# Row layout of the first 512 tokens and new engine orders in a fused linear-attention and ReLU kernel

## The chip, the cores and the metric

The kernel runs on one core of one Trainium2 chip. The metric is device time in microseconds (us), as the median of plain runs. Beside them there is one execution with the hardware profiler on; rows of the profile come from that one.

## What is computed

Two blocks read the same x of 2048 tokens by 512 (A_x; the input B_x is not used), and a gate per token mixes them. All tensors are bf16.

```python
x = A_x
g = sigmoid((x * gate_w).sum(-1, keepdims=True))
# a: 32 heads of 16; q, k, v = x @ wqkv
pq = q @ w_phi; pk = k @ w_phi                      # per head
phi_q = concat(softmax(pq), softmax(-pq))           # 32 features per head
phi_k = concat(softmax(pk), softmax(-pk))
kv = sum over tokens of phi_k * v;  z = sum over tokens of phi_k
a = ((phi_q @ kv) / (phi_q @ z + 1e-6)) @ wo
# b: b = max(x @ w1, 0) @ w2                         (w1 512 x 1376, w2 1376 x 512)
out = g * a + (1 - g) * b
```

The order of tokens matters nowhere except that a row of the output belongs to the same row of x: the sums over tokens don't depend on it.

## The kernel before, in words

**Tiles.** The 2048 tokens are 16 tiles of 128, in four chunks of 512. XT holds x transposed (512 features on partitions in four blocks, tokens along the row). The first chunk is loaded plainly (two loads, xa0 and xa1, each with two neighbouring rows of x per partition, lines 277 to 282) and transposed on PE (xt0a to xt3b, line 325; copied out by ACT and DVE, xe, lines 337 and 339). The other three chunks come by transposing loads (x1, x2, x3, line 269). Tile m of the first chunk thus holds every second row of a block of 256, and the function rows(m) writes the output of these tiles back to the same rows (line 348).

**The steps,** with the names that the text uses, a number standing for a tile, job or chunk:

- v (line 374): values of a tile, copied out by ACT (ve, 379).
- f1, f0 (356): w_phi folded into the key and query weights; these weights come by transposing loads wkT and wqT. Evictions fe (317, 319).
- h (397): x @ w1, one block of 128 hidden features by 512 tokens, ReLU by ACT into HT (rl, 415). The last 96 features and the gate's dot product come in hr (405), with rr on ACT and a transposing load ht (426) from SBUF to SBUF.
- pr (454): the folded projection of a job (two tiles, or one at the end; k0 to k8 for keys, q0 to q8 for queries). Then ev (ACT, 479), mx and mn (DVE, 483, 485), t1 and t2 (POOL, 492), ex (ACT, 497), sm and rc (DVE, 499, 503, 523), and nm (POOL, 506 for keys, 529 for queries; ra at 525 before it).
- kv (513): sum of key features by values over all tokens in two PSUM banks; kn and kz (544, 546) copy it out once kv15 is done.
- tq (532): transposing load of a query tile's features; nd (556): numerator and denominator in two halves; rd and o (562, 564) divide and gate; to (569): transposing load of that into OT.
- b (577): HT @ W2 of a tile, eleven matmuls, and a (583): OT @ WO, four matmuls into the same PSUM bank; oe (628) evicts with the factor 1 - g, and st (631) stores, both on ACT. The last tile is split into two parts (598, 609, 619, 622).

**What sets the order.** Each step is a task with an engine and dependencies. Nothing is scheduled when the kernel runs: the dictionary ORDER (line 17) holds the order of every engine's queue, written out: sp (all loads, 54), pool, act, dve and pe. `emit` (127) goes through each queue and puts a semaphore wait ahead of a task whose dependencies lie on other engines. A task that waits holds up all behind it on its engine. The numbers `dur` and `lat` of the tasks are not used to build the program.

**Buffers that tie engines together.** The h units, hr and f0 take the PSUM banks 3, 4, 5 in turn by their number (h0_0 bank 3, h0_1 bank 4, h0_2 bank 5, h0_3 bank 3, and so on); each waits for the eviction of the one before it in that bank. The v of tiles 4 to 15 share bank 2. b and a of tile m use bank 3, 4 or 5 and wait for oe of tile m - 3. nd uses banks 6, 7 and 2 in turn and waits for the o three halves before. Each pr waits for the ev before it (banks 0 and 1).

```python
for s, v in need.items():
    if waited.get(s, 0) < v:
        waited[s] = v
        eng.wait_ge(sems[s], v)
last = t.fn(eng)
last.then_inc(sems[t.sem], 16 if t.dma else 1)
```

Of the kernel before, what the change touches and what calls it, by code (L numbers as in the profile page):

```python
# [15 lines left out]

ORDER = {
    "sp": (
        "xa0 wva xa1 wvb w1a wphi wkT w1b x1 gw w1c wqT x2 x3 w2a w2b ht1 wo ht0 tq1 tq0 tq2 tq3 to0 to1 ht2 to2 "
        "tq4 tq5 to3 tq6 tq7 to4 to5 ht3 tq8 tq9 to6 to7 tq11 tq10 to8 to9 tq12 tq13 to11 to10 tq14 tq15 to12 "  # L20
        "to13 to14 to15 st15_1 "
    ),
    "pool": (
# [5 lines left out]
    ),  # L29
    "act": (  # L30
# [8 lines left out]
    ),  # L39
    "dve": (  # L40
# [10 lines left out]
    ),  # L51
# [10 lines left out]
    ),  # L62
}

# [78 lines left out]
def bass_gated_mix__linear_kernel_hedgehog__dense_activation_relu__prompt_kernel(  # L143
# [11 lines left out]
    x2 = A_x.rearrange("b s d -> (b s) d")  # L155
    o2 = out.rearrange("b s d -> (b s) d")
# [3 lines left out]
    P = 128  # L160
# [20 lines left out]
    with ExitStack() as es:  # L181
# [92 lines left out]

        w1r = B_w1.rearrange("(j p) n -> p j n", p=P)
        wvr = A_wqkv[:, 2 * D:3 * D].rearrange("(j p) n -> p j n", p=P)
        def pair(i):
            return x2[2 * i * P:2 * (i + 1) * P, :].rearrange("(p t) d -> p (t d)", t=2)

        load("xa0", "sp", XN[:, 0:2, :].rearrange("p t d -> p (t d)"), pair(0), dur=0.47, lat=2.25)  # L280
        load("wva", "sp", WV[:, 0:2, :], wvr[:, 0:2, :], dur=0.46, lat=2.55)
        load("xa1", "sp", XN[:, 2:4, :].rearrange("p t d -> p (t d)"), pair(1), dur=0.5, lat=3.2)
        load("wvb", "sp", WV[:, 2:4, :], wvr[:, 2:4, :], dur=0.48, lat=3.75)
        load("w1a", "sp", W1[:, :, 0:512], w1r[:, :, 0:512], dur=0.51, lat=4.75)
# [62 lines left out]

        def rows(m):
            if m < 4:
                i = m // 2  # L350
                return o2[2 * i * P:2 * (i + 1) * P, :].rearrange("(p t) d -> p t d", t=2)[:, m % 2, :]
            return o2[m * P:(m + 1) * P, :]

        def pe_fold(q, s, j, b):
# [105 lines left out]
        for jn, (kind, tiles) in enumerate(jobs):  # L460
# [27 lines left out]
            for tn, M, sg in (("t1", MX, 0), ("t2", MN, 1)):  # L488
                o3 = ap(TS, NTS * 2 * F, ts * 2 * F + sg * GV, [[2 * GV, w * NG], [DH, GH], [1, DH]])
                m3 = ap(M, NSL * 2 * H, sl * 2 * H, [[GH, w * NG], [1, GH], [0, DH]])  # L490
                a3, b3 = (pb3, m3) if sg == 0 else (m3, pb3)
# [27 lines left out]
            else:  # L519
# [29 lines left out]
                for m in tiles:  # L549
# [38 lines left out]
                    if m == NT - 1:  # L588
# [41 lines left out]
                        (f"a{m}", f"go{m // 4}", f"st{m - NOS}" if m >= NOS else None), dur=0.69)  # L630
                    add(f"st{m}", "act", lambda q, m=m: q.dma_start(
                        out=rows(m), in_=OSB[:, m % NOS, :]), (f"oe{m}",), dur=0.39, lat=1.7, dma=True)

        for line in (("warm0", "xt0a", "xt0b", "xt1a", "xt1b", "v0a", "v1a", "xt2a", "xt2b", "xt3a", "xt3b", "warm1",
# [45 lines left out]
```

## Time and profile before

| | before |
|---|---|
| median of 3 plain runs | 151.71 us |
| lowest, highest | 151.42, 151.90 us |
| the profiled execution | 151.17 us |
| its span, first to last instruction | 149.2 us |
| PE, DVE, POOL, ACT busy | 97%, 74%, 74%, 61% |
| TensorE clock granted | 1.00 |
| read from and written to HBM | 4.41 MB, 2.10 MB |

A row of a group or of a timeline names the line of the kernel, the engine, the operation, and out<-in by the program's tensors. PE is the matmul side of TensorE, PEld its weight loads, SPq the queue of SyncE that issues loads. In the chain of work that ended last, each piece has a start, a length and what it was; "issue" is time for which the profile shows no cause. Times are counted from the span's start.

### The profile page before, as it was taken

What the parts mean: (1) busy time and instruction counts of PE and PEld (TensorE: products, weight loads), DVE (VectorE), ACT (ScalarE), POOL (GpSimd) and SP (SyncE); (2) the same over time, 40 slices, a digit from 0 to 9 for tenths busy, and PEclk for the clock granted to TensorE, in tenths of its full rate; (3) what the DMA queues carried; (4) which work ended last, traced back from release to release, by engine and by line L of the source; (5) the groups of instructions that cost most, each with busy time, mean ns of one, the idle gap of its engine ahead of it and who ended that gap; (6) DMA issues with size and microseconds to landing.
All of it is one profiled execution on the core that took longest, in us unless ns stands there. A gap on an engine that the chain in (4) does not pass through costs nothing.

```text
span 149.2 us, 2538 instructions
## 1 busy us (share of the span) xinstructions
PE 144.9 (97%) x968; PEld 73.0 (49%) x984; DVE 110.8 (74%) x169; ACT 91.1 (61%) x127; POOL 109.7 (74%) x73
## 2 busy tenths in 40 slices
PE   7899999999999999999999999999999999999994
PEld 2454444454454645444547445444545454544553
DVE  0542679999995499989569899999979987817501
ACT  3347769997886888966896854476535443303131
POOL 4000599999999999999999999999958795060000
PEclk9999999999999999999999999999999999999999
DMA  5999999500003400000000061847495964787423
GB/s 140 295 199 223 259 166 276 191 0 0 4 2 94 116 7 0 0 0 0 4 0 0 0 141 32 151 104 186 102 172 109 245 156 107 135 208 211 106 73 108
DMA packets 45524, 16.11 MB, mean 108 GB/s; under 512 B 39272, under 2 KB 45256, under 8 KB 45512
## 3 DMA queue, kind: packets, MB, share of 16 engines
q1 hardware_dynamic: 43208, 13.89, 42.3%
q10 hardware_dynamic: 2304, 2.06, 4.3%
q8 instruction: 8, 0.13, 0.4%
q14 instruction: 4, 0.03, 0.1%
HBM read 4.41 MB, written 2.10 MB: 44 GB/s over the span
## 4 chain that ended last, share of the span: by engine, by line
PE 94%; DMA 3%; issue 1%; SPq 1%; DVE 0%
PE PS L577 24%; PE PS L397 23%; PE PS L454 19%; PE PS L374 9%; PE PS L583 9%; PE PS L513 3%; DMA FT<-in_A_x_dram 3%; PE PS L556 3%; PE PS L405 2%; PE PS L598 2%; PE PS L356 1%; PE PS L609 1%; SPq L265 1%; PE PS L325 0%; DVE OSB L619 0%
## 5 line engine op out<-in xcount | busy, mean ns | idle before, releaser
L492 POOL TENSOR_TENSOR TS<-PB,MX 128x1024 bf16<-128x1024 bf16 (+1 forms) x18 | 30.8, 1716 | 13.9 <-DVE MX L483 13.9
L499 DVE TENSOR_REDUCE ZB<-FT 128x128 f32<-128x2048 bf16 (+1 forms) x18 | 36.6, 2037 | 4.6 <-ACT FT L497 4.5
L397 PE MATMUL PS<-XT,W 128*128 128x512 bf16 x155 | 37.7, 379 | 0.3
L577 PE MATMUL PS<-W,HT 128*128 128x512 bf16 (+1 forms) x161 | 37.0, 379 | 0.2
L497 ACT ACTIVATE FT<-TS 128x2048 bf16<-128x2048 bf16 (+1 forms) x18 | 31.0, 1720 | 4.5 <-PE PS L513 2.4
L492 POOL TENSOR_TENSOR TS<-MN,PB 128x1024 bf16<-128x1024 bf16 (+1 forms) x18 | 30.8, 1720 | 0.1
L454 PE MATMUL PS<-WP,XT 128*128 128x512 bf16 x126 | 30.1, 379 | 0.1
L506 POOL TENSOR_TENSOR FT<-FT,SC 128x2048 bf16<-128x2048 bf16 (+1 forms) x9 | 29.5, 3285 | 0.0
L415 ACT ACTIVATE HT<-PS 128x512 bf16<-128x512 f32 x40 | 22.8, 601 | 6.3 <-PE PS L397 6.2
L628 ACT ACTIVATE OSB<-PS,OMG 128x512 bf16<-128x512 f32 x15 | 10.2, 685 | 23.5 <-PE PS L583 23.5
L479 ACT ACTIVATE PB<-PS 128x1024 bf16<-128x1024 f32 (+1 forms) x18 | 16.8, 932 | 12.3 <-PE PS L454 8.1
L577 PEld LDWEIGHTS PS<-W,HT 128*128 128x128 bf16 (+1 forms) x165 | 15.5, 97 | 17.4 <-ACT OSB L628 0.3
L397 PEld LDWEIGHTS PS<-XT,W 128*128 128x128 bf16 x160 | 15.0, 98 | 17.5 <-ACT HT L415 1.0
L483 DVE TENSOR_REDUCE MX<-PB 128x64 bf16<-128x1024 bf16 (+1 forms) x18 | 19.5, 1082 | 5.4 <-ACT PB L479 5.4
L485 DVE TENSOR_REDUCE MN<-PB 128x64 bf16<-128x1024 bf16 (+1 forms) x18 | 19.2, 1075 | 0.3 <-ACT PB L479 0.2
L454 PEld LDWEIGHTS PS<-WP,XT 128*128 128x128 bf16 x128 | 12.1, 98 | 14.0 <-DVE WP L319 0.4
L529 POOL TENSOR_TENSOR FT<-FT,SR 128x1024 bf16<-128x1024 bf16 (+1 forms) x9 | 15.6, 1736 | 0.6
L374 PE MATMUL PS<-WV,XT 128*128 128x512 bf16 x61 | 15.5, 379 | 0.2
L583 PE MATMUL PS<-WO,OT 128*128 128x512 bf16 x58 | 14.4, 378 | 0.1
L564 DVE SCALAR_TENSOR_TENSOR OTM<-PS,EG,RD 128x256 bf16<-128x256 f32 x32 | 14.1, 466 | 0.4
L562 DVE RECIPROCAL RD<-PS 128x16 f32<-128x16 f32 x32 | 7.0, 238 | 8.2 <-PE PS L556 7.9
L379 ACT ACTIVATE VS<-PS 128x512 bf16<-128x512 f32 x16 | 9.5, 607 | 3.0 <-PE PS L374 3.0
(54 smaller groups left out, 96.3 us busy)
## 6 DMA issues: line engine op xcount, KB each, us to landing
out_dram<-OSB ACTq DMA_DIRECT2D x15, 128.0 KB, 2.5
W<-in_B_w_dram SPq DMA_DIRECT2D x1, 1280.0 KB, 8.2
W<-in_B_w_dram SPq DMA_DIRECT2D x2, 512.0 KB, 5.0
FT<-in_A_x_dram SPq DMA_DIRECT2D x2, 256.0 KB, 3.4
WV<-in_A_wqkv_dram SPq DMA_DIRECT2D x2, 256.0 KB, 3.7
WO<-in_A_wo_dram SPq DMA_DIRECT2D x1, 512.0 KB, 4.6
W<-in_B_w_dram SPq DMA_DIRECT2D x1, 352.0 KB, 3.6
PHQ<-FT SPq DMA_TRANSPOSE x16, 2.8
```

Of the source, the lines that this page charges most:

```text
L374: last = q.matmul(PS[:, b, :], XT[:, j, m * P:(m + 1) * P], WV[:, j, :], start=(j == 0), stop=(j == ND - 1))
L397: last = q.matmul(PS[:, b, :], W1[:, j, k * P:(k + 1) * P], XT[:, j, chunk(c)], start=(j == 0), stop=(j == ND - 1))
L415: add(f"rl{a}_{k}", "act", lambda q, a=a, k=k, b=b: q.activation(HT[:, k, chunk(a)], PS[:, b, :], ACT.Relu), (f"h{a}_{k}",), dur=0.6)
L454: last = q.matmul(PS[:, n, :], XT[:, j, m * P:(m + 1) * P], WP[:, s, j, :], start=(j == 0), stop=(j == ND - 1))
L483: add(f"mx_{J}", "dve", lambda q, sl=sl, w=w, i=pbg: q.tensor_reduce(MX[:, sl, 0:w * H], i, AX.X, ALU.max), (f"ev_{J}", old("t1")), dur=0. ...
L485: add(f"mn_{J}", "dve", lambda q, sl=sl, w=w, i=pbg: q.tensor_reduce(MN[:, sl, 0:w * H], i, AX.X, ALU.min), (f"ev_{J}", old("t2")), dur=0. ...
L492: add(f"{tn}_{J}", "pool", lambda q, o3=o3, a3=a3, b3=b3: q.tensor_tensor(o3, a3, b3, ALU.subtract), (f"{'mx' if sg == 0 else 'mn'}_{J}", ...
L497: add(f"ex_{J}", "act", lambda q, fs=fs, ts=ts, w=w: q.activation(FT[:, fs, 0:w * F], TS[:, ts, 0:w * F], ACT.Exp), (f"t1_{J}", f"t2_{J}", ...
L499: add(f"sm_{J}", "dve", lambda q, fs=fs, sl=sl, w=w: q.tensor_reduce(ZB[:, sl, 0:2 * w * H], FT[:, fs, 0:w * F].rearrange("p (g d) -> p g ...
L506: add(f"nm_{J}", "pool", lambda q, f3=f3, sl=sl, w=w: q.tensor_tensor(f3, f3, SC[:, sl, 0:2 * w * H].unsqueeze(2).to_broadcast([P, 2 * w * ...
L577: last = q.matmul(PS[:, ab, :], HT[0:r, k, m * P:(m + 1) * P], W2[0:r, k, :], start=(k == 0), stop=False)
L583: last = q.matmul(PS[:, ab, :], OT[:, m % NOT, t, :], WO[:, t, :], start=False, stop=(t == ND - 1))
```

## The change

Two things. First, the 512 tokens of the first chunk are laid out with four neighbouring rows of x per partition instead of two: partition p holds rows 4p to 4p + 3, xa0 loads the rows 4p and 4p + 1, xa1 the rows 4p + 2 and 4p + 3. Each load has 128 pieces of 2,048 bytes as before, now 4,096 bytes apart instead of one behind the other; tile m < 4 holds the rows 4p + m, and its output goes back to these rows, 1,024 bytes each, 4,096 instead of 2,048 bytes apart.

```diff
+        first = x2[0:4 * P, :].rearrange("(p t) d -> p t d", t=4)
+
         def pair(i):
-            return x2[2 * i * P:2 * (i + 1) * P, :].rearrange("(p t) d -> p (t d)", t=2)
+            return first[:, 2 * i:2 * (i + 1), :].rearrange("p t d -> p (t d)")
...
         def rows(m):
             if m < 4:
-                i = m // 2
-                return o2[2 * i * P:2 * (i + 1) * P, :].rearrange("(p t) d -> p t d", t=2)[:, m % 2, :]
+                return o2[0:4 * P, :].rearrange("(p t) d -> p t d", t=4)[:, m, :]
             return o2[m * P:(m + 1) * P, :]
```

Second, the orders of all five queues are replaced. The tasks, their shapes and their dependencies are the same; lines after 277 move down by two or one. The first 16 loads on SP stay, then:

```diff
 "sp" (from ht1)
-ht1 wo ht0 tq1 tq0 tq2 tq3 to0 to1 ht2 to2 tq4 tq5 to3 tq6 tq7 to4 to5 ht3 tq8 tq9 to6 to7 tq11 tq10 to8 to9
-tq12 tq13 to11 to10 tq14 tq15 to12 to13 to14 to15 st15_1
+ht1 ht0 tq0 ht2 wo tq1 tq2 tq3 to0 to1 to2 tq4 tq5 to3 ht3 tq6 to4 tq7 tq9 tq8 to5 to6 to7 tq10 to8 tq11 tq12
+to9 tq13 to10 tq14 tq15 to11 to12 to13 to14 to15 st15_1
 "pool" (from nm_k8)
-nm_k8 ra_q1 nm_q1 t1_q3 t2_q3 t1_q4 ra_q2 nm_q2 t2_q4 t2_q5 ra_q3 nm_q3 t1_q5 t1_q6 ra_q4 nm_q4 t2_q6 ra_q5 nm_q5
+nm_k8 ra_q1 nm_q1 t1_q3 t2_q3 t1_q4 ra_q2 nm_q2 t2_q4 ra_q3 nm_q3 t1_q5 t2_q5 ra_q4 nm_q4 t2_q6 t1_q6 t1_q7 t2_q7
 "act" (start, and the stores)
-xe00 xe10 xe20 xe30 ve1 ve2 ve3 fe1_1 fe1_3 ve0 rl0_0 ev_k0 rl0_3 rl0_1 rl0_2 ev_k1
+xe00 xe10 xe20 xe30 ve1 rl0_0 fe1_3 fe1_1 ve3 ve2 rl0_3 ev_k0 rl0_6 rl0_1 ev_k1
-oe5 gp2 ex_q6 st2 st4 st0 gp3 oe6 ex_q7 oe7 ex_q8 st7 oe8 oe9 st9 st8 oe10 oe11 st5 st6 st10 st11 oe12 oe14
+oe4 st3 ex_q6 ex_q7 oe5 ev_q8 oe6 oe7 ex_q8 oe8 st4 st1 st6 st2 oe9 st9 oe10 st5 oe11 st10 st7 st11 oe12 oe13
 "pe" (start; from pr_q5)
-v3b h0_0 f1_0 f1_1 f1_2 f1_3 h0_1 pr_k0 h0_3 h0_2 pr_k1
+v3b h0_0 f1_0 f1_3 f1_2 f1_1 h0_3 pr_k0 h0_6 h0_1 pr_k1
-pr_q5 h3_2 h3_9 h3_5 b2 kv14 h3_8 kv15 b1 nd0_1 nd1_0 nd0_0 pr_q6 nd1_1 b0 nd2_1 nd2_0 pr_q7 nd3_0 a0 nd3_1 a1
-b3 b4 a2 nd5_0 nd4_0 a3 nd4_1 b5 nd5_1 b6 pr_q8 nd6_1 nd6_0 a4 nd7_0 a5 nd7_1 b7 b8 nd8_0 nd9_0 nd8_1 a6 a7 nd9_1
-b9 nd10_0 b10 a8 nd11_0 nd11_1 nd10_1 a9 b11 b12 nd12_1 nd12_0 a10 a11 nd13_0 nd13_1 nd14_0 b13 nd15_0 nd14_1 a12
-nd15_1 b14 a13 a14 b15 a15_0 a15_1
+pr_q5 h3_2 b2 h3_5 h3_9 kv14 h3_8 kv15 b1 nd0_0 nd0_1 pr_q6 nd1_1 nd1_0 b0 nd2_0 nd2_1 pr_q7 nd3_0 a0 nd3_1 a1
+b3 b4 nd4_0 nd4_1 a2 a3 nd5_0 nd5_1 b5 b6 nd6_0 nd6_1 a4 pr_q8 nd7_1 nd7_0 b7 nd8_0 a5 nd8_1 nd9_0 a6 b8 nd9_1 b9
+a7 a8 nd10_1 nd10_0 b10 nd11_1 b11 nd11_0 a9 nd12_0 a10 nd12_1 nd13_0 b12 nd14_0 nd13_1 nd14_1 b13 nd15_1 a11
+nd15_0 a12 b14 a13 a14 b15 a15_0 a15_1
```

Between these parts the queues of POOL, ACT, DVE and PE also change places among near neighbours. The beginning of PE up to h0_0 and its end from a13 on are as before.

More of the change, by code (lines that the diff above doesn't have):

```diff
@@ L18 @@
     "sp": (
-        "xa0 wva xa1 wvb w1a wphi wkT w1b x1 gw w1c wqT x2 x3 w2a w2b ht1 wo ht0 tq1 tq0 tq2 tq3 to0 to1 ht2 to2 "
-        "tq4 tq5 to3 tq6 tq7 to4 to5 ht3 tq8 tq9 to6 to7 tq11 tq10 to8 to9 tq12 tq13 to11 to10 tq14 tq15 to12 "
+        "xa0 wva xa1 wvb w1a wphi wkT w1b x1 gw w1c wqT x2 x3 w2a w2b ht1 ht0 tq0 ht2 wo tq1 tq2 tq3 to0 to1 to2 "
+        "tq4 tq5 to3 ht3 tq6 to4 tq7 tq9 tq8 to5 to6 to7 tq10 to8 tq11 tq12 to9 tq13 to10 tq14 tq15 to11 to12 "
         "to13 to14 to15 st15_1 "
```

62 rows, old and new, of the table ORDER are left out of this document.

## The prediction

> **What bounds the kernel now.** I read three parts of the page first: busy time, the 40 slices, and the chain that ended last; then the pieces of that chain in order of time; then the SP queue's instructions.
>
> ```profile
> PE 144.9 (97%) x968; PEld 73.0 (49%) x984; DVE 110.8 (74%) x169; ACT 91.1 (61%) x127; POOL 109.7 (74%) x73
> ...
> PE 94%; DMA 3%; issue 1%; SPq 1%; DVE 0%
> ```
>
> PE is busy 97% of the span and holds 94% of the chain. A busy share alone does not say that an engine is the bound, so the pieces of the chain decide:
>
> ```profile
> 1.67 4.13 DMA FT<-in_A_x_dram
> 5.81 0.05 issue
> 5.85 0.62 PE PS L325 x8
> ...
> 9.38 0.87 PE PS L397 x4
> 10.24 0.01 issue
> 10.25 1.07 PE PS L356 x16
> ...
> 26.11 1.73 PE PS L454 x8
> 27.84 1.73 PE PS L397 x8
> ...
> 120.01 1.73 PE PS L583 x8
> ...
> 146.14 0.89 PE PS L609 x8
> 147.03 0.03 issue
> 147.06 0.38 DVE OSB L619
> ```
>
> The reader is to see three stretches. Until 5.81 us the chain is the second load of x (xa1, issued at 1.67, 4.13 us to land). From 5.85 to 147.03 it is PE without a break: eight 512-column matmuls always take 1.73 us (216 ns each), and the pieces follow each other; the 0.05 us pieces called issue lie between two halves of one group whose sum with them is the usual one (81.85 to 83.58 is 1.73), so they are missing records, not idle time. After 147.03 come 0.4 us of eviction and one store. Inside the PE stretch I looked for tasks longer than their kind: the first fold (16 matmuls in 1.07 us against 4 x 0.22 = 0.89) and the first projection after it (1.84 against 1.73) are the only ones above 0.1 us. So an order can win at most 0.3 us inside the stretch in this execution.
>
> **Baseline.** The profiled execution took 151.17 us: span 149.2, and 1.97 around it. The plain runs have a median of 151.71 (151.42 to 151.90), 0.54 above. I work the sum against 151.17 and add 0.54 at the end.
>
> **Part 1, the rows.** xa0 and xa1 still move 128 pieces of 2,048 B each; only their pitch in memory goes from 2 KB (one solid block) to 4 KB. The packet records of the trace give the price: 256 packets of 2,048 B, median 84 ns. A strided read stands beside it: WV and W1 come in 1,024 B pieces out of rows 3,072 and 2,752 B long, median 46 ns, so 92 ns for 2,048 B. Each of the 16 DMA engines carries 16 of the x packets: 16 x 84 = 1.34 us. At the strided price it would be 16 x 92 = 1.47, that is +0.13 us on xa1, and PE waits for xa1, so all of it would count. On the other side nothing is to be won: the first fold needs the transposed key weights (wkT), which landed at 10.20, and PE came to it at 10.24; an earlier xa1 gains at most 0.04. Range -0.04 to +0.13; I take 0.0, since a 2,048 B packet stays one packet. The stores of tiles 0 to 3 write the same 1,024 B rows at 4 KB instead of 2 KB pitch: 46 ns a packet today, hidden under PE (ACT issues them, none is waited for before its OSB slot is used again eight tiles later); 0.
>
> **Part 2, the orders.** The matmuls are the same on both sides, form by form (160 of h, 128 of the projections, 165 + 22 of b, 60 + 8 of a, and so on), so PE's sum is unchanged and the orders can only add or remove waits. I went along the five new queues adding the rows' durations (two-tile POOL steps 1.91 and 3.67 us, less the 0.04 by which neighbours overlap; h 0.86, b 2.38, a 0.86, nd 0.13, kv 0.26 on PE; SP 1.2 to 1.35 per transposing load). Where a margin below is tight, this is the sum:
>
> - Start of h0. The new order uses bank 3 for h0_0, h0_3 and h0_6 in turn. ACT does rl0_0 (from 10.26), fe1_3, fe1_1, ve3, ve2, rl0_3, each about 0.6 less 0.1 of overlap: rl0_3 ends at about 13.6. PE reaches h0_6 at 11.32 + 0.86 (h0_3) + 1.73 (pr_k0) = 13.9 to 14.0. Margin 0.4; if ACT were a step later, 0.2 lost.
> - kv15. POOL has no idle time from 16.4 to nm_k8 in either order, and the set of steps ahead of nm_k8 is the same (18 t of k, 9 nm, 6 t of q0 to q2, ra_q0, nm_q0): 14 x 1.87 + 4 x 1.00 + 7 x 3.63 + 2 x 1.90 + 6 x 1.87 + 0.28 + 1.89 = 72.8, so 89.2 to 89.35. PE also has the same set ahead of kv15, 89.67. Margin 0.3, unchanged.
> - a6, the tightest of the new places. Behind a6 stand on PE b8 to b14 (7 x 2.38), b15 2.41, nine a (7.78), a15 0.89 and 13 nd (1.66): 29.4 in all, so it starts at 147.03 - 29.40 = 117.6; before it started at 120.0, because b8 is now behind it. Its input to6: POOL ends nm_q4 at 89.35 + 10 x 1.88 + 4 x 0.28 = 109.3 (up to 109.8 with small waits); SP then issues tq9, tq8, to5, to6 at steps of 1.35, 1.27 and 1.23, so to6 at 113.2 to 113.8. With the median of 2.4 us it lands at 115.6 to 116.2: margin 1.4.
> - a9 and a10: by the same count PE comes to them at 130.4 and 131.4; to9 and to10 are issued at about 124.1 and 126.7. Margins 3.9 and 2.3 at the median.
>
> The landing times of these loads are what is uncertain:
>
> ```profile
> 115.79 2.65 SPq L569 DMA_TRANSPOSE OT<-OTM  x2
> ```
>
> This row of the SP queue (start, time on the queue) is to6 and to7. All 16 loads of their kind, from the rows of OT:
>
> ```profile
> DMA to landing us min/median/max: 2.3/2.4/4.4
> ```
>
> to6 took 3.92 us: ACT issued three stores between 114.98 and 115.86. to9 took 4.41, beside a 16 KB instruction packet of 1.14 us at 125.57. Other transposing loads without such company took 2.3 to 2.4. With 3.92 the new a6 has a margin of -0.1 to +0.5, with 4.41 of -0.6 to 0.0. The new order issues four stores (st4 st1 st6 st2) in a row after oe8, beside to10; with 4.41 a10 keeps 0.3. I take 2.4 to 2.9 for to6, since only st3 is near it now, and no wait: 0.0 (range 0.0 to +0.6). *DMA: Bandwidth & Descriptors* of the Trainium skill, section "Queues, rings and completion order", says that a DMA engine serves the queues that have work in turn, packet by packet; to6's 3.92 beside stores agrees. By that rule alone a late to6 needs stores to move with it, not before it.
>
> A gain below nothing in this part: in the profiled execution margins were already enough, so at most the 0.3 of the folds, which both orders keep (f1_0 still waits for wkT, pr_k0 for the last of four evictions). Beside moved transposes: wo moves on SP from 45.6 to about 86.4, behind tq0 and ht2; it lands about 4.6 us later, at 91, and a0 is at 98.2. Behind it waits tq1, needed at about 94.
>
> Sum: 151.17 + 0.0 (rows) + 0.0 (orders) = 151.2 for a profiled execution, 151.7 as a median of plain runs.
>
> **Rivals.**
> 1. *No change* (the forecast): the row order changes no packet and no order changes PE's sum. 151.7, own range 151.3 to 152.15. For it: the unbroken chain. Against: the 0.54 us between the profile and the plain runs has no explanation in the page.
> 2. *Faster*: those 0.54 us are PE waits on late transposing loads, which the profiled execution just escaped. It had to6 at 119.71 for PE at 120.01 (0.30), to9 at 127.80 for 127.99 (0.19), to1 at 98.72 for 99.16 (0.44); a landing 0.5 later costs 0.2, 0.3 and 0.1, together about 0.6. The new order gives a6 1.4, a9 3.9, a10 2.3. Then 151.71 - 0.5 = 151.2. Against: the same 0.54 may sit in xa1 and wkT, where nothing is changed.
> 3. *Slower, xa1*: reads at 4 KB pitch are slower. PE stands until xa1 lands, and POOL, ACT and DVE start behind it, so every tenth moves the end by a tenth. It decides from 112 ns a packet (16 x 28 = 0.45 us). At half the rate, 168 ns, it is +1.34: 153.0; at 120 ns, +0.6: 152.3. For it: nothing in the rows beyond the 92 ns. The same page of the Trainium skill, "Latency and other measured facts", reports copies at 207 GB/s and less when the rows of the partitions lie 512 KiB or more apart at a power of two. No run here shows it, and 4 KB is far from it; an estimate by halving would be the 153.0.
> 4. *Slower, a6*: to6 lands 4.4 us or more after its issue, because st3 or an instruction packet meets it. It decides at 3.8 us; with 4.4 the wait is up to 0.6: 152.3.
>
> **How the numbers follow.** About 0.3% (0.45 us) is what a measurement of this kernel can tell from no change. No change 0.52, rival 2 faster 0.24, rival 3 0.13, rival 4 0.11. Hence faster 0.24, same 0.52, slower 0.24. The time is the forecast's 151.7. The range takes in rival 2 (151.2, less 0.3 for the spread of runs) and rivals 3 and 4 at 152.3 plus as much: 150.9 to 152.6; left out are xa1 at half rate and an order that hides more than the profile shows.
>
> **What would show it.** Right: xa1 lands near 5.8 us, the chain is PE from there to the end at 216 ns a matmul, and the last matmul ends near 147.0. Part 1 wrong: x packets well above 84 ns, xa1 later, everything behind it shifted. Part 2 wrong: PE idle ahead of a6 (L583) on a DMA of OT, or ahead of kv15 on POOL, or ahead of h0_6 on ACT. Rival 2 right: no new gap and the same profile, but the plain runs come down to about 151.2. What would make all of it wrong is a wait that I put at nothing in the first 85 us, where PE and ACT exchange buffers with margins of 0.2 to 0.4 us.

## The result and the profile after

The changed kernel takes 152.81 us (152.10 to 153.11, 8 runs) against 151.45 us (150.76 to 151.90, 8 runs): ratio 1.0083, interval 1.0062 to 1.0104. It is slower by 1.36 us; the prediction was no change, 151.7 us, with a range up to 152.6. The three runs from which the prediction took its 151.71 are among the eight of the kernel before. A second set of runs of the two kernels gave a smaller loss, 1.0051 (1.0029 to 1.0073), 0.84 us.

The profiled execution of the changed kernel took 153.11 us, its span is 151.8. First come two rows of its page: the busy time of each engine, and the engines' shares of the chain that ended last.

```profile
PE 146.1 (96%) x967; PEld 73.6 (49%) x984; DVE 111.2 (73%) x169; ACT 91.3 (60%) x127; POOL 109.6 (72%) x73
...
PE 86%; DMA 10%; issue 1%; DVE 1%; SPq 1%; DVEq 0%
```

Busy shares hardly move. The chain does: PE had 94% of it and has 86%, DMA had 3% and has 10%. The pieces of the chain in order of time (start, length, what) show where the DMA comes in:

```profile
1.67 4.79 DMA FT<-in_A_x_dram
6.46 0.05 issue
...
95.01 4.11 DMA OT<-OTM
99.13 0.14 issue
99.26 1.02 PE PS L584 x4
...
127.73 5.70 DMA OT<-OTM
133.43 0.05 issue
133.47 1.04 PE PS L584 x4
...
148.40 0.89 PE PS L610 x8
149.29 0.02 issue
```

Three pieces are new or longer. The first load of x's second half landed at 6.46 instead of 5.81 us. Two transposing loads of OT lie on the chain: to0 (95.01, 4.11 us) ahead of a0, and to10 (127.73, 5.70 us) ahead of a10. The longest landing of these loads (rows of OT) was 4.4 us before, and is now that of to10:

```profile
DMA to landing us min/median/max: 2.3/2.4/5.7
```

PE's own waits say how much of that was idle time (engine, line, who ended it: us in total, times, longest):

```profile
PE PS L584 <- DMA OT<-OTM: 1.3, 2, 0.9
```

Counted by the time between the ends of tasks, a10 took 1.89 us where four matmuls take 0.86 (+1.03), and a0 1.51 (+0.64). That is some 0.3 us more than the 1.3 us of idle time: after an idle stretch the four matmuls themselves last 1.02 and 1.04 us from the first start to the last end. PE's last matmul ended at 149.29 instead of 147.03, +2.26: 1.03 + 0.64 + about 0.6 that it already had after the first projection (ended 14.63 instead of 14.02). Nothing else in the 143 us of PE is longer than before.

What lay beside to10 can be read in the rows of the timeline around it (start, time, engine, line, operation):

```profile
126.41 0.95 ACTq L632 DMA_DIRECT2D out_dram<-OSB  x2
...
127.40 1.17 ACTq L632 DMA_DIRECT2D out_dram<-OSB  x2
...
127.73 1.19 SPq L570 DMA_TRANSPOSE OT<-OTM  x1
...
133.47 0.82 PE L584 MATMUL PS<-WO,OT 128*128 128x512 bf16 x3 [0.86 <-DMA OT<-OTM]
```

The four stores st4, st1, st6, st2 were issued between 126.41 and 128.57; to10 was issued among them, at 127.73. The packet records of the trace add a third party. The page lists a DMA queue of kind "instruction" with eight packets of 16,384 B in the whole execution; they are called instruction packets here. One of them ran from 128.96 for 1.82 us (the page counts a packet as work of one of the 16 DMA engines). The 256 B pieces of the transposing loads near it, 18 ns in the median, took up to 2.04 us.

**Theories.** T1: the loss is the late landing of to10, and at times of to0, beside stores and an instruction packet. T2: the 4 KB pitch of x (the distance between the pieces that neighbouring partitions read) makes the first loads late. T3: the new orders lose in some other way.

### The profile page after: what moved, and what is told of

Same layout as the page of the kernel before. It is cut to its first block, busy times and chain, and to the rows that moved or that the text cites. A ratio compares the mean times of both kernels' runs of the same rounds, so it can differ in the third digit from the quotient of the medians.

```text
span 151.8 us, 2540 instructions
## 1 busy us (share of the span) xinstructions
PE 146.1 (96%) x967; PEld 73.6 (49%) x984; DVE 111.2 (73%) x169; ACT 91.3 (60%) x127; POOL 109.6 (72%) x73
## 3 DMA queue, kind: packets, MB, share of 16 engines
HBM read 4.41 MB, written 2.10 MB: 43 GB/s over the span
## 4 chain that ended last, share of the span: by engine, by line
PE 86%; DMA 10%; issue 1%; DVE 1%; SPq 1%; DVEq 0%
PE PS L398 23%; PE PS L578 19%; PE PS L455 18%; PE PS L375 9%; PE PS L584 8%; DMA OT<-OTM 6%; DMA FT<-in_A_x_dram 3%; PE PS L514 3%; PE PS L557 2%; PE PS L406 2%; PE PS L599 2%; PE PS L357 1%; PE PS L610 1%; SPq L265 1%; PE PS L327 0%
## 5 line engine op out<-in xcount | busy, mean ns | idle before, releaser
L375 PE MATMUL PS<-WV,XT 128*128 128x512 bf16 x63 | 16.8, 395 | 0.1
```

What stands on the lines that cost most here:

```text
L375: last = q.matmul(PS[:, b, :], XT[:, j, m * P:(m + 1) * P], WV[:, j, :], start=(j == 0), stop=(j == ND - 1))
```

## The experiments

Ratios are to runs of the kernel before on the same chip, with their 95% intervals. "Wait of a10" is the time of that task above 0.86 us in the profile of that kernel.

**Rows alone.** The kernel before with its own ORDER; `pair` and `rows` alone are replaced, as in the first cut of the change.

> The old orders with four neighbouring rows per partition. Theory 1 (the loss is late landing of moved transposing loads, to0 and to10, beside stores and instruction packets): nothing but noise, ratio 0.998 to 1.003, xa1 lands at 5.6 to 6.5 us from run to run. Theory 2 (reads of x at 4 KB pitch are slow: xa1 at 6.46 instead of 5.81): +0.4 us or more, ratio 1.003 to 1.006, with xa1 near 6.4 us and the rest of the chain as before.

Measured: 151.57 against 151.45 us, 1.0012 (0.9989 to 1.0035). xa1 landed at 6.58, wkT at 10.81. The time speaks for T1; the landings looked like T2, so the same kernel was profiled a second time.

> The old orders with four rows once more, for a second profile. Theory 1: xa1 at 5.6 to 6.5 us and not twice at the same late value. Theory 2: xa1 near 6.4 us again.

Measured: one run of 151.76 us; xa1 at 5.79, but wkT at 10.95 and the first projection's end at 14.77. xa1 was not late again, wkT was. That left T2 open.

**Pitch of 16 KB.** The kernel before with four times the pitch of the change. Its first 512 tokens are then other rows of x than their outputs belong to; the loads and all the work keep their sizes.

```diff
-            return x2[2 * i * P:2 * (i + 1) * P, :].rearrange("(p t) d -> p (t d)", t=2)
+            return x2.rearrange("(p t) d -> p t d", t=16)[:, 2 * i:2 * (i + 1), :].rearrange("p t d -> p (t d)")
```

> The old orders; the two loads of x read rows 16p to 16p + 3 (pitch 16 KB instead of 2 KB, the same 2,048 B pieces). The first 512 tokens are therefore computed from other rows of x, and their outputs are not those of the reference; the work is the same. If the pitch in memory slows the first loads, a pitch four times that of the change must show it at least as much: xa1 and w1a or wkT 0.5 us or more later than 5.8, 8.2 and 10.2, ratio 1.003 to 1.010. If the 4 KB runs were only late by chance: ratio 0.998 to 1.002 and wkT anywhere from 10.2 to 10.9.

**The kernel before, once more.**

> The kernel before once more, for a second profile and for what two sets of runs of one kernel differ by. Ratio 0.998 to 1.002. If the layout is what makes the first loads late, wkT lands at 10.1 to 10.4 us and xa1 near 5.8; if that was chance, wkT may lie anywhere up to 10.9.

Measured: pitch 16 KB 1.0013 (1.0003 to 1.0023), with xa1 at 5.91 and wkT at 10.65; the kernel before itself 0.9988 (0.9974 to 1.0002), with xa1 at 6.69 and wkT at 11.20, later than any four-row profile. So the start differs between executions of one kernel by a full microsecond (the first projection ended at 14.02 and 15.02). In the second profile of the kernel before, PE's waits (engine, line, who ended it: us in total, times, longest) show it:

```profile
PE PS L325 <- DMA FT<-in_A_x_dram: 1.1, 1, 1.1
```

Over all profiles but that of the 16 KB pitch, the first projection ended at 14.02 to 15.02 us with two rows (six profiles, mean 14.45) and at 14.39 to 14.77 with four (seven, mean 14.56). The layout costs 0.1 us, if anything; even the 16 KB pitch costs about 0.2. T2 can't be the loss.

**Orders alone.** The new ORDER, the old rows.

> The new orders with two rows per partition. Theory 1: nearly the whole loss, ratio 1.006 to 1.011, with PE idle ahead of a10 or a0 on a DMA of OT. Theory 2: half or less, ratio 1.002 to 1.005, with xa1 near 5.8 us.

Measured: 152.00 us, 1.0047 (1.0025 to 1.0070); a10 waits 0.93 us on to10, which landed 5.60 us after its issue; a0 doesn't wait. The ratio itself lies in the range given for T2, and its interval reaches into that for T1, so it did not decide; the wait ahead of a10 is T1's. The changed kernel and this one were run again on one chip.

> The changed kernel once more, on one chip with the three below and with a second profile. If its loss is the wait ahead of a10 and now and then one ahead of a0: ratio 1.005 to 1.009, a wait ahead of a10 of 0.7 to 1.1 us in the profile, the one ahead of a0 (0.64 in the first profile) not always there.

> The new orders with two rows once more, beside the changed kernel on one chip: the difference of the two is the layout alone. If the 2,048 B pieces cost the same at both pitches: within 0.002 of the changed kernel. If the layout is a third of the loss: 0.003 to 0.005 below it.

Measured: 1.0051 (1.0029 to 1.0073) with four rows and 1.0060 (1.0038 to 1.0083) with two; a10 waits 0.76 and 0.69 us; a0 waits 0.26 with four rows. The rows make no difference to the loss that these runs can tell.

**The stores apart.** In the changed kernel, ACT issues the four stores earlier:

```diff
-... st3 ex_q6 ex_q7 oe5 ev_q8 oe6 oe7 ex_q8 oe8 st4 st1 st6 st2 oe9 ...
+... st3 ex_q6 ex_q7 oe5 st4 st1 st2 ev_q8 oe6 st6 oe7 ex_q8 oe8 oe9 ...
```

> The changed kernel with its four stores st4 st1 st6 st2 issued earlier (three after oe5, one after oe6) and not beside to10. Theory 1: to10 lands in 2.4 to 3.5 us instead of 5.7, no wait ahead of a10, about 0.8 to 1.0 us faster than the changed kernel: ratio to before 1.001 to 1.004. Theory 3 (something in the new orders other than landings): no better than the changed kernel, 1.006 to 1.010.

Measured: 151.55 us, 1.0012 (0.9991 to 1.0033). The rows of this kernel's timeline:

```profile
127.04 1.19 SPq L570 DMA_TRANSPOSE OT<-OTM  x1
...
130.78 1.02 PE L584 MATMUL PS<-WO,OT 128*128 128x512 bf16 x4
...
131.77 1.02 PE L584 MATMUL PS<-WO,OT 128*128 128x512 bf16 x4
```

The first is to10, the two others a9 and a10: a10 starts as soon as a9 and the nd between them are done. to10 is still the longest of its kind (rows of OT), at 3.90 us:

```profile
DMA to landing us min/median/max: 2.3/2.4/3.9
```

That is not the 2.4 to 3.5 expected; the instruction packet (128.10, 1.41 us) is still beside it. PE came to a10 4.7 us after its issue, so that cost nothing. The changed kernel did not run on this chip, but the new orders with two rows did, at 152.00 us: moving four stores on an engine that is 60% busy takes back nearly all of that loss. T3 had 1.006 to 1.010 and is out as the main cause.

**The code packet moved.** The code packet is the instruction packet near 129 us. In the changed kernel, two waits that are already met ahead of each of 40 tasks of PE. The trace records 40 more instructions on PE for them, in all 69 semaphore waits instead of 29. They bring the later instruction packets forward.

```diff
+            if e == "pe" and 20 <= order[e].index(t) < 60:
+                eng.wait_ge(sems["pool"], 1)
+                eng.wait_ge(sems["pool"], 2)
             last = t.fn(eng)
```

> The changed kernel with 40 more instructions on PE between h0 and kv (waits that are already met), so that PE's instruction packets come some 4 us earlier: near 125 instead of 129 us, ahead of the four stores and of to10. If both stores and packet are needed: to10 lands in 3 to 4.5 us, wait ahead of a10 0 to 0.3 us, about 0.7 us faster than the changed kernel, ratio 1.002 to 1.006. If the stores alone do it: to10 above 5 us again and ratio 1.006 to 1.010.

Measured: the packet came at 124.22 us instead of 128.96; to10 landed after 4.22 us and a10 did not wait. 151.99 us, 1.0033 (1.0008 to 1.0058), with runs from 151.12 to 153.05. The profile says that packet and stores are both needed; the time says that a loss of 0.5 us remains, with a spread that one profile can't explain (the profiled execution, 151.25 us, was the second fastest of the twelve). The orders alone lost 0.55 us in their set, so the packet's part is shown by the landing of to10 and not by the time.

**The same in the kernel before.** Four stores in a row beside to9 and the packet near 125.6 us:

```diff
-... gp2 ex_q6 st2 st4 st0 gp3 oe6 ex_q7 oe7 ex_q8 st7 oe8 ... oe11 st5 st6 ...
+... gp2 ex_q6 st0 gp3 oe6 ex_q7 oe7 ex_q8 st2 st4 st5 st7 oe8 ... oe11 st6 ...
```

> The kernel before with four stores (st2 st4 st5 st7) in a row after ex_q8, beside to9 and the instruction packet near 125.6 us. Theory 1 (four stores and an instruction packet beside one transposing load make it land over 5 us after its issue): to9 lands in 5 to 6 us instead of 4.4, PE waits ahead of a9 0.5 to 1.2 us, ratio 1.003 to 1.008. Theory 3 (the loss belongs to the new orders in another way): 0.998 to 1.002.

Measured: 0.9995 (0.9983 to 1.0006), no wait, so the expected time was missed. The load that both delayed was not to9, which landed at 126.64, after 2.97 us, 0.7 us into the packet (125.98, 1.82 us). It was the next one, tq12: issued at 125.70, landed 5.36 us later, as the longest of its kind (rows of PHQ):

```profile
DMA to landing us min/median/max: 2.7/2.8/5.4
```

PE came to its nd 5.1 us after it had landed in the first profile of the kernel before (133.64 against 128.55), so nothing waited. A load of this kind takes 2.8 us in the median, so the delay is 2.6 us, somewhat less than the 3.0 to 3.3 of to10. What a delay costs depends on the margin of the load that it hits.

**wo early.** The changed kernel with wo right after ht1, as before.

> The changed kernel with wo issued right after ht1, as before, in place of after ht2. If the late wo holds up tq1 and the code packet of PE (96.0 us in the first profile, 92 in others) and so to0: tq1 lands in 2.7 to 3.3 us instead of 4.9, no wait ahead of a0, 0.1 to 0.4 us faster than the changed kernel; the wait ahead of a10 stays. If wo has no part in it: the same as the changed kernel within 0.15%.

Measured: 1.0072 (1.0043 to 1.0100). tq1 lands in time again (the longest of PHQ is 3.7 instead of 4.9 us), a0 doesn't wait, a10 waits 0.94 us. The late tq1 was wo's doing and cost no time that these runs can tell.

**Two rows, stores apart and wo early.**

> Two rows, the new orders, the four stores earlier (as in the kernel with stores apart) and wo issued early as in the kernel before. If the landings beside stores, code packets and wo are all of the loss: ratio 0.997 to 1.001, no wait ahead of a0 or a10. If the new orders lose elsewhere: 1.002 or more.

Measured: 151.43 against 151.43 us, 1.0000 (0.9981 to 1.0019). a10 doesn't wait; a0 waited 0.25 us here, with a packet at 95.85. So wo early doesn't prevent that. On this chip the three kernels of the new orders with the stores beside to10 took 152.27 to 152.39 us: neither the rows nor wo alone changed that, and with the stores moved the loss is gone. By the interval at most 0.3 us is left for T3. No order tried beats the kernel before.

The landing of to10 in all these profiles of the new orders:

| kernel | stores beside | packet at, us | to10 issued | us to landing | wait of a10 |
|---|---|---|---|---|---|
| changed | yes | 128.96 | 127.73 | 5.70 | 1.03 |
| orders alone | yes | 128.15 | 126.59 | 5.60 | 0.93 |
| changed again | yes | 128.41 | 127.14 | 5.43 | 0.76 |
| two rows again | yes | 128.54 | 127.00 | 5.36 | 0.69 |
| wo early | yes | 128.40 | 126.84 | 5.62 | 0.94 |
| stores apart | no | 128.10 | 127.04 | 3.90 | 0 |
| stores apart, wo early | no | 128.49 | 127.35 | 3.93 | 0 |
| code packet moved | yes | 124.22 | 127.06 | 4.22 | 0 |

An undisturbed one takes 2.4. The packet without stores adds 1.5, the stores without this packet 1.8, both together 3.0 to 3.3, about their sum. A second instruction packet, of 8,192 B and at most 0.6 us, runs during to10's flight in all eight kernels (at 127.7 to 128.8 us): it is part of every row, and what it adds is not known. The mean wait of the five kernels with both is 0.87 us; the mean difference of their medians from the kernel before is (1.36 + 0.55 + 0.84 + 0.96 + 0.96) / 5 = 0.93 us. Kernel by kernel the two don't match so well (0.93 against 0.55 for the orders alone, 0.69 against 0.96 for two rows again): a wait is of one execution, a difference of a set of runs.

## Why the prediction was wrong

- **What bounds the kernel:** right. PE's sum is the same on both sides, and every tenth of a wait on PE shows in the end.
- **Part 1, the rows:** borne out as far as can be told. It took 0.0 in a range up to +0.13; the starts of 13 profiles differ by 0.1 in their means, two profiles of one kernel by 1.0.
- **Part 2, a6:** right. to6 was issued at 115.05, landed 2.38 us later, and PE came to a6 about 1.5 us after that; the prediction had 1.4 for it.
- **Part 2, a10: the step that failed.** The prediction saw the four stores beside to10 and wrote that "with 4.41 a10 keeps 0.3". The margin was right: it gave to10 4.7 us from issue to use, and the profile gives 4.9. The landing was mis-sized: 4.41 was the longest in the old trace, and it was taken as the upper end. That trace held the two delays nearly apart: 3.92 beside three stores and no packet, 4.41 beside an instruction packet and one store (st7, in flight from 123.61 to 126.16, which the prediction doesn't name). The new order brings four stores and a packet on one load: 2.4 + (3.92 - 2.4) + (4.41 - 2.4) = 5.9, against 5.36 to 5.70 measured; the sum is somewhat too high, as one store is in both terms. Added up, these rows of the old trace would have given a wait of about 1.2 ahead of a10, and 152.9 us by the prediction's own base.
- **The instruction packet** was named, for a6, in rival 4, and not placed. The last three came at 107.69, 125.57 and 144.57 us before, at 109.11, 128.96 and 146.98 after. The new orders moved to10 from 130.51 to 127.73 and the packet from 125.57 to 128.96, and so brought them together. Rival 4 had the kind of mechanism and a price of 0.6; its place was wrong.
- **a0:** of its inputs the prediction considered wo and tq1, not to0. When a packet comes at 95.8 to 96.0 (three profiles) to0 takes 3.7 to 4.1 us and a0 waits 0.25 to 0.64; when it comes at 92.3 to 92.6 (four profiles), or at 86.7 with the packet moved, a0 doesn't wait. What puts it at the one or the other time stays open; the early wo is not it.
- **Rival 2:** wrong. The 0.54 us between the old profile and its plain runs was no loss at transposing loads: the second profile of the kernel before has no wait ahead of any a, and its start is a microsecond later. With the median of eight runs, 151.45, only 0.28 of the 0.54 is left.
- **Rival 3:** did not occur, though the changed kernel's profile, taken alone, showed it (xa1 0.65 us later).

Open: what sets the time of the packet ahead of to0, what the 8,192 B packet adds, and how the plain runs of the kernel with the moved packet come to spread over 1.9 us.

## What to carry to other kernels

A margin at a transfer is held against the sum of the delays that its neighbours can cause, not against the longest landing in a trace where they hardly met. When an order moves a critical transfer, look at what the other queues issue in the same 4 us, stores of an idle engine and the instruction packets of the busy one too; here moving four stores was worth nearly the whole loss. And take a second profile before a 0.6 us difference in the first loads is put down to a change.

## What the runs showed of the hardware

The instruction packets were the surprise. One of 16,384 B comes on average every 124 weight loads of PE (84 to 169 between two of them) and takes 0.9 to 1.8 us. A transposing load of OT that was in flight when it came, with no store beside, took 3.7 to 4.3 us instead of 2.4 (12 loads in seven profiles; to10 in the kernel with the stores apart is one of them, with 3.90). Forty added instructions on PE moved the packet of interest by more than 4 us, which shows that these packets belong to PE. *DMA: Bandwidth & Descriptors* of the Trainium skill, "Queues, rings and completion order", says that a DMA engine switches between queues only when a packet is done; the trace agrees in part. Five 256 B pieces of more than 1.7 us started while the packet of 1.82 us ran (at 129.97 to 130.29) and ended together, at 132.01 to 132.03; but the packet was over at 130.78, and the rule does not say what held them for another 1.2 us. In the prediction the same rule was read for stores alone.
